# At the turn between the two parities: the last down matmuls ahead of the first key product, and the last chunk's weight sums two places sooner

## The chip, the cores and the metric

The kernel runs on one core of a Trainium2 chip. The metric is the device time of one execution in microseconds (us). The work is done by TensorE (PE in the profile; PEld is its weight load), VectorE (DVE), ScalarE (ACT), GpSimd (POOL) and SyncE (SP). POOL and SP here do hardly anything but issue DMA transfers.

## The reference

Out of one input x (2048 tokens, 512 wide) two branches are computed, and mixed per token by a gate.

```
def _A_ref(x, wqkv, wo):                      # 32 heads of 16, window of 8 tokens, every second one
    qkv = (x @ wqkv) -> q, k, v
    idx = pos[:, None] - 2 * arange(8)[None, :]
    logits = einsum("bhsd,bhswd->bhsw", q, k[idx]) * scale      # masked where idx < 0
    return einsum("bhsw,bhswd->bhsd", softmax(logits), v[idx]) @ wo

def _B_ref(x, w_gate, w_up, w_down):          # 1792 hidden columns
    return (gelu(x @ w_gate) * (x @ w_up)) @ w_down

g = sigmoid((x * gate_w).sum(-1))
return g * _A_ref(x, wqkv, wo) + (1 - g) * _B_ref(x, w_gate, w_up, w_down)
```

## The kernel before

**Parities.** The attention looks back over every second token, so the tokens are dealt into two halves of 1024, here called parities (`par` 0 and 1). The program runs in this order: `start()` makes the keys and queries of the first parity, `ffn(0)` makes its values and its whole feed-forward branch, `kq_second()` makes the keys and queries of the second parity, `ffn(1)` does the rest. The place where `ffn(0)` goes over into `kq_second()` is the turn.

**Products.** Each fp32 operand is split in a rounded part (`hi`) and the rest (`lo`), and a product is three matmuls: hi by hi, lo by hi, hi by lo. A group of products in two by two blocks is done with seven block products in place of eight (the names `a11`, `s1`, `t1` and so on are the block operands, where `s` and `t` are sums of blocks). An operand is made by one ScalarE copy for `hi` and one VectorE subtraction for `lo`. In `kq_second()` one such block product is `block(...)`: 24 matmuls. Its first is `a11` by `b11` into the four PSUM banks `acc0` to `acc3` (called `U`); ScalarE then copies the four banks into four banks of the tag `p` (called `V_`), and the second product, `a12` by `b21`, goes on top of these. The third, `s2` by `t2`, goes on top of `U`.

**Feed-forward.** `ffn(par)` goes over 14 chunks `f` of 128 hidden columns. `gate_up` does the seven products of a chunk, and between them, at nine places numbered 0 to 8, the steps that were put there with `at(place, step)`: fetches of later chunks' weights, sums of weight blocks (`combine`), their splits (`operands`, `down_w`), and pieces of the down product of the chunks before. The seventh product of a chunk (`last`, `a22` by `t4`) is done in the next chunk. `hidden` then makes gelu(gate) times up and splits it into `hh` and `hl`: a VectorE multiplication, a ScalarE rounding, a VectorE subtraction. `down` multiplies a pair of chunks' `hh` and `hl` with the down weights. Its tiles `b` = 0 stand in the banks `acc0` to `acc3` and its tiles `b` = 1 in `p` banks; at the last pair both are copied out with the scale `gc` (line 613), which frees the banks.

**Weights of a chunk, first parity.** Two chunks ahead, `fetch(f + 2)` loads the four weight blocks into a `raw` tile, and `combine(f + 2)` makes the sums `t1`, `t3`, `t2`, `t4` in place by three VectorE subtractions (line 499): first `t1` and `t3` in one instruction, then `t2`, then `t4`. One chunk ahead, `operands(par, f + 1, i)` makes, for the group of blocks `i` = 0 (`t1`, `t2`, `b11`) and `i` = 1 (`b21`, `t3`, `t4`, `b22`), a negated rounded copy on ScalarE (line 517), adds the raw weights to it by a DMA that accumulates, issued from POOL (line 518: `lo` is what this DMA leaves), and makes the rounded copy itself on ScalarE (line 522). So line 517 waits for `combine`, line 518 for line 517, and the first product of the chunk for the landing of line 518.

**What sets the order.** A scheduler decides the order of the instructions on each engine from a priority (the order in which the code records them) and its own estimate of times. The code bends it by hand: `paced(ins)` makes an instruction wait for the matmul recorded last; `ordered(a, b)` only fixes that `a` stands behind `b` on the same engine, with no semaphore. The helpers `row`, `act` and `mms` chain what is recorded through them on VectorE, ScalarE and TensorE in the order of the code; `mms` chains the matmuls of `block`. The attention itself (lines 325 to 401, VectorE for the most part) is a generator, `fill`, from which pieces are pulled in between at a lower priority.

**The turn.** After the chunks, `ffn(0)` records the last pair's `down` tiles, `b` = 0 and then `b` = 1, and after each of them one step of `ready()`, which makes operands for the second parity: `s12` sums, `b21`, `s1` and so on. Then `kq_second()` begins with its first block. In the built program, in which the down matmuls and the chained block matmuls bear no order to each other, the scheduler put the last twelve down matmuls (those of the 14th chunk's `hh` and `hl` by its down weights, four `p` tiles) behind the first block.

Of the kernel before, what the change touches and what calls it, by code (L numbers as in the profile page):

```python
# [12 lines left out]
AF = mybir.ActivationFunctionType  # L13
OP = mybir.AluOpType
# [8 lines left out]
FC = F // P  # L23
# [26 lines left out]
def tile_gated_mix(ctx: ExitStack, tc: tile.TileContext, xt, wqkv, wff, wo, out):  # L50
    nc = tc.nc
# [10 lines left out]
    def tl(tag, dt=F32):  # L62
        return pool.tile([P, COLS.get(tag, 512)], dt, name=tag, bufs=BUFS[tag])
# [12 lines left out]
    LAST, SCORED, PEAK, LESS = [], [], [], []  # L76
# [195 lines left out]
    def values(par):  # L272
        steps = [value_steps(par, t) for t in range(BT)]
        for chunk in PLAN:
            for place in chunk:
                for n in place.split():
                    steps[int(n[1])][n[0]]()
                    pull(0.77)
                if n == "g3":
                    done.add((par, 1))  # L280
                yield
# [127 lines left out]
    def after(ins, other, cls=mybir.DependencyClass.Sync):  # L409

        tc.add_manual_dep(ins.ins, other.ins.name, mybir.DependencyInfo(cls, mybir.DependencyReason.SCHED_ONLY),
                          reason="pace")

    def paced(ins):
        after(ins, LAST[-1])

    def ordered(ins, other):
        after(ins, other, mybir.DependencyClass.NoSync)
# [85 lines left out]
    def operands(par, f, i):  # L504


        n = len(GROUPS[i]) * QW
        w = tl(f"g{i}", F32R)
        hi, lo = w[:, :n], w[:, n:2 * n]
        for k, op in enumerate(GROUPS[i]):  # L510
            WG[f, op] = hi[:, k * QW:(k + 1) * QW], lo[:, k * QW:(k + 1) * QW]
        if par and not i:
            nc.sync.dma_start(w[:, :2 * n].bitcast(F32), WS[f, i])
            yield
            return
        raw = RAW[f][:, (0, 4)[i] * QW:][:, :n]
        nc.scalar.activation(lo, raw, AF.Copy, scale=-1.0)  # L517
        nc.gpsimd.dma_start(lo.bitcast(F32), raw, accum_op=OP.add)  # L518
        if not i:
            KEEP[f] = w[:, :2 * n]  # L520
        yield
        ins = nc.scalar.activation(hi, raw, AF.Copy)  # L522
        if f:
            paced(ins)

    def keep(f):

        WS[f, 1] = dram.tile([P, 2 * QW], F32, name=f"ws{f}1")
        paced(nc.sync.dma_start(WS[f, 1], RAW[f][:, 5 * QW:7 * QW]))
# [40 lines left out]
        return s  # L570

    def hidden(key, ge, up):
        nc.vector.tensor_tensor(ge, ge, up, op=OP.mult)  # L573
        hh_, hl_ = tl("hh", F32R)[:, :512], tl("hl", F32R)[:, :512]
        nc.scalar.activation(hh_, ge, AF.Copy)  # L575
        nc.vector.tensor_tensor(hl_, ge, hh_.bitcast(F32), op=OP.subtract)  # L576
        Hs[key] = hh_, hl_

    late, COPIED = [], []

    def pace(par, f):
        return PACE[2 if par else f > 5]
# [122 lines left out]
    def ffn(par):  # L705
        XOP.update(((n, kc), X[par, blk, kc + k]) for n, blk, k in (("a11", 0, 0), ("a12", 0, 2), ("a22", 1, 2))
                   for kc in range(2))
        todo, extra = iter(()), values(par)
        for f in range(FC):
            do = {}  # L710

            def at(i, x, *args):
                do.setdefault(i, []).append(lambda: x(*args))

            if f > 1:
                pieces = [[lambda b=b, i=i: down(par, f // 2 - 1, f % 2 * 2 + i, b)] for b in range(2) for i in range(2)]
            else:
                pieces = [()] * 4
            if f + 1 < FC:
                for i in range(2):  # L720
                    steps = operands(par, f + 1, i)
                    at(1 + 2 * i - (not par and f == 1), next, steps, None)
                    at(5 + i - (not par and f == 1), next, steps, None)
                if f:
                    at(0 if f != 1 else 7 if par else 5, fetch_d, f + 1)
                else:
                    for g_ in range(2):
                        at(6 + g_, fetch_d, g_)
                if f == 1:
                    for g_ in range(2):  # L730
                        at(3, down_split, g_)
                if f in (2, 3) and not par:
                    at(3 if f == 2 else 1, down_split, f)
                elif f > 1:
                    steps = down_w(f)
                    at(0 if f % 2 and not par else 2, next, steps, None)
                    at(7, next, steps, None)
            else:
                steps = down_w(f)
                at(1, next, steps, None)  # L740
                at(4, next, steps, None)
            if par:
                if f + 2 < FC:
                    at(0, fetch_sums, f + 2)
                else:
                    at(0, fetch_o) if f + 2 == FC else None
                if f + 1 == FC:
                    todo = chain(load_o(), channels_of(0, 0))
                    for i in range(1, 9):
                        at(i, next, todo, None)  # L750
            else:
                if f + 2 < FC:
                    at(1, fetch, f + 2)
                    at((4, 5, 6)[f] if f < 3 else 8, combine, f + 2)
                else:
                    at(0, fetch_x, 1, f + 2 - FC)
                if f + 1 < FC:
                    do.setdefault(0, []).insert(0, lambda: keep(f + 1))
                at(0, keep_parts, f)
                if f + 1 == FC:  # L760
                    todo = before()
                    for i in range(2, 9):
                        at(i, next, todo, None)
            gate_up(par, f, pieces, do, extra if f < 2 else iter(()))
        for _ in todo:
            pass
        fourth()
        if par:
            out_first()
            oT = {}  # L770
        else:
            Q2["mark"] = LAST[-1]
            Q2["turn"] = ready()
        for b in range(2):
            for t in range(BT):
                down(par, NG - 1, t, b)
                if par and t == 0:
                    oT[0, b] = channels(par, 0, b)
                if not par:
                    next(Q2["turn"], None)  # L780
        if par:
            finish(oT)
# [117 lines left out]
    row, act, mms = Row(nc.vector), Row(nc.scalar), Row(nc.tensor)  # L900
# [5 lines left out]
    SRC, OP_, Q2, RAWS = {}, {}, {}, {}  # L906
# [15 lines left out]
    def hi(n, k):  # L922
        return act.activation(OP_[n, k][0], SRC[n, k], AF.Copy)
# [16 lines left out]
    def block(ps, a, w, first, kcs=(0, 1), ask=0.0):  # L940
        for t in range(BT):
            for kc in kcs:
                ah, al = OP_[a, kc]
                wh, wl = OP_[w, kc]
                for n, (a_, w_) in enumerate(((ah, wh), (al, wh), (ah, wl))):
                    mm(ps[t], t, a_, w_, first and kc == 0 and n == 0, kc == 1 and n == 2)
            if ask:
                pull(ask)
# [275 lines left out]
    def ready():  # L1224

        q = Q2["q"] = [[XR[k][:, i * 512:(i + 1) * 512] for i in range(4)] for k in range(2)]
        load_pairs("t2")
        name("t3", pairs(slots("g0", 3) + slots("c", 1)), halves(RAWS["b12"]))
        yield
        hi("a12", 1)  # L1230
        lo("a12", 1)
        s12 = Q2["s12"] = [tl("r") for _ in range(2)]
        for n in ("s1", "s2", "s3", "s4"):
            for k in range(2):
                XOP[n, k] = pair("S")
            name(n, [XOP[n, k] for k in range(2)], s12 if n in ("s1", "s2") else [q[k][n == "s4"] for k in range(2)])
        name("a22", [X[1, 1, 2 + k] for k in range(2)], [q[k][3] for k in range(2)])
        for k in range(2):
            after(row.tensor_tensor(s12[k], q[k][2], q[k][3], op=OP.add), Q2["mark"])
        paced(hi("b21", 0))  # L1240
        lo("b21", 0)
        yield
        paced(hi("b21", 1))
        lo("b21", 1)
        yield
        both(hi, "s1")
        both(lo, "s1")
        yield
        for k in range(2):
            sub(s12[k], s12[k], q[k][0])  # L1250
        yield
        sub(RAWS["b12"], RAWS["b22"], RAWS["b12"])
        yield

    def kq_second():
        for _ in Q2["turn"]:
            pass
        q, s12 = Q2["q"], Q2["s12"]
        t4 = slots("g1", 4)
        name("t4", pairs(t4), halves(RAWS["b21"]))  # L1260
        U = [bank(f"acc{t}") for t in range(BT)]

        block(U, "a11", "b11", True, ask=ASK[0])
        V_ = [bank("p") for _ in range(BT)]
        for t in range(BT):
# [142 lines left out]
```

## Time and profile before

| | |
|---|---|
| Time, median of 3 runs | 598.41 us (597.75 to 599.1) |
| The profiled execution: its own time | 600.29 us |
| The profiled execution: span from first to last instruction | 598.5 us |
| Mean granted TensorE clock | 0.997 |
| Busy DVE / ACT / POOL | 539.8 / 389.7 / 87.6 us |
| HBM read / written | 68.30 / 38.86 MB |

Times in the views are microseconds from the span's start. In the views, `out<-in` names the tile written and the tiles read, `x4` is a count of merged instructions, and the bracket at a row's end is the time for which the engine was idle before it and what it waited for. The end of a matmul is modelled and reaches into the next one; the distance from one start to the next is the safe measure of its cost.

### The profile page before, as it was taken

The page shows a single profiled execution, that of the slowest core. Times are in us where ns is not written, and L with a number is a line of the kernel's source. Part 1 is how long each engine was busy: PE and PEld are TensorE (multiplying, and loading weights), DVE is VectorE, ACT ScalarE, POOL GpSimd, SP SyncE. Part 2 cuts the span into 40 slices and gives each one's busy share as a digit, 9 for nine tenths or more (in the row PEclk, how much of TensorE's full clock was granted, in tenths as well). Part 3 has the DMA queues.
Part 4 walks back from the last instruction along what each step waited for, and adds up shares of the span by engine and source line. Part 5 has one row for each costly group of instructions (what it writes and reads, how often), then busy time and mean ns, then how long its engine had stood idle before and what let it go on. Part 6 is the DMA issues. An engine that isn't in the chain of part 4 may idle for free.

```text
span 598.5 us, 8098 instructions
## 1 busy us (share of the span) xinstructions
PE 588.5 (98%) x2730; PEld 489.1 (82%) x2730; DVE 539.8 (90%) x646; ACT 389.7 (65%) x676; POOL 87.6 (15%) x119
## 2 busy tenths in 40 slices
PE   9999999999999999899899999999999999999997
PEld 6888988888888788787788988888788888888886
DVE  5998999879999899799899999998999999999972
ACT  5857656597677876686784446767656756695532
POOL 0501101021212121101108001111111111101200
PEclk9999999999999999999899999999999999999999
DMA  8778989788998898988669898876878878737834
GB/s 314 248 232 233 275 268 284 221 207 255 239 286 221 223 263 216 236 275 301 213 184 263 253 267 199 246 219 160 214 183 214 209 203 237 221 96 204 127 67 158
DMA packets 79522, 133.65 MB, mean 223 GB/s; under 512 B 7932, under 2 KB 45178, under 8 KB 79224
## 3 DMA queue, kind: packets, MB, share of 16 engines
q1 hardware_dynamic: 64426, 98.72, 50.6%
q0 software_dynamic: 12288, 32.45, 27.4%
q10 hardware_dynamic: 2766, 1.96, 1.0%
q8 instruction: 21, 0.34, 0.2%
q14 instruction: 21, 0.17, 0.1%
HBM read 68.30 MB, written 38.86 MB: 179 GB/s over the span
## 4 chain that ended last, share of the span: by engine, by line
PE 90%; DMA 3%; ACT 2%; DVE 2%; issue 2%; SPq 0%; POOL 0%; POOLq 0%; ACTq 0%; DVEq 0%
PE p L560 41%; PE p L602 11%; PE acc L602 11%; PE acc L898 7%; PE acc L211 7%; PE p L898 6%; PE p L831 5%; PE acc L831 2%; DMA g<-raw 2%; DMA prod<-wqkv 1%; DVE prod L388 1%; ACT g L517 0%; ACT L345 0%; ACT rt L613 0%; ACT L657 0%
## 5 line engine op out<-in xcount | busy, mean ns | idle before, releaser
L560 PE MATMUL p<-S,g 128*128 128x512 f32 x672 | 168.0, 390 | 0.6 <-DVE s L569 0.6
L560 PEld LDWEIGHTS p<-S,g 128*128 128x128 f32 x672 | 125.7, 188 | 26.9 <-DVE s L569 1.0
L560 PE MATMUL p<-A,g 128*128 128x512 f32 x504 | 128.8, 390 | 1.8 <-DMA g<-raw 1.8
L560 PEld LDWEIGHTS p<-A,g 128*128 128x128 f32 x504 | 93.5, 188 | 21.3 <-DMA g<-raw 2.3
L328 DVE TENSOR_REDUCE lg<-prod 128x128 f32<-128x2048 f32 x32 | 72.9, 2278 | 0.1
L518 POOL DMA_DIRECT2D g<-raw x40 | 34.5, 862 | 244.8 <-ACT g L517 130.7
L602 PE MATMUL p<-d,hh 128*128 128x512 f32 x224 | 68.3, 391 | 0.2 <-ACT p L596 0.2
L602 PE MATMUL acc<-d,hh 128*128 128x512 f32 x224 | 61.1, 389 | 0.0
L388 DVE TENSOR_TENSOR prod<-kq,lg 128x2048 f32<-128x2048 f32 x24 | 54.6, 2273 | 2.0 <-PE p L602 1.1
L602 PEld LDWEIGHTS p<-d,hh 128*128 128x128 f32 x224 | 41.7, 188 | 10.2 <-ACT p L596 1.7
L602 PEld LDWEIGHTS acc<-d,hh 128*128 128x128 f32 x224 | 42.1, 188 | 8.6
L565 ACT ACTIVATE s<-p 128x512 f32<-128x512 f32 x56 | 33.2, 596 | 24.3 <-PE p L560 24.0
L522 ACT ACTIVATE g<-raw 128x1024 fp32r<-128x1024 f32 (+1 forms) x40 | 39.5, 988 | 12.8 <-PE p L560 9.6
L618 ACT ACTIVATE rt<-p 128x512 f32<-128x512 f32 x48 | 27.7, 592 | 24.9 <-PE p L602 24.6
L569 DVE TENSOR_TENSOR s<-p,s 128x512 f32<-128x512 f32 x56 | 37.9, 680 | 6.0 <-PE p L560 5.4
L576 DVE TENSOR_TENSOR hl<-c,hh 128x512 fp32r<-128x512 f32 x56 | 38.1, 680 | 4.4 <-ACT hh L575 4.2
L602 PE MATMUL p<-d,hl 128*128 128x512 f32 x112 | 42.0, 389 | 0.0
L573 DVE TENSOR_TENSOR c<-c,s 128x512 f32<-128x512 f32 x56 | 38.1, 681 | 2.9 <-ACT c L676 2.9
L575 ACT ACTIVATE hh<-c 128x512 fp32r<-128x512 f32 x56 | 35.1, 626 | 8.7 <-DVE c L573 8.4
L517 ACT ACTIVATE g<-raw 128x1024 fp32r<-128x1024 f32 (+1 forms) x40 | 39.3, 986 | 1.3 <-DMA raw<-wff 0.5
L392 DVE TENSOR_TENSOR prod<-prod 128x1024 f32<-128x1024 f32 x32 | 38.9, 1216 | 0.2
L547 POOL DMA_DIRECT2D d<-r x22 | 18.9, 857 | 130.3 <-ACT d L546 93.2
(205 smaller groups left out, 1021.1 us busy)
## 6 DMA issues: line engine op xcount, KB each, us to landing
g<-raw POOLq DMA_DIRECT2D x27, 512.0 KB, 7.2
raw<-wff SPq DMA_DIRECT2D x42, 256.0 KB, 3.7
ws<-g SPq DMA_DIRECT2D x14, 768.0 KB, 6.3
g<-ws SPq DMA_DIRECT2D x14, 768.0 KB, 6.1
r<-wff SPq DMA_DIRECT2D x28, 256.0 KB, 4.0
d<-r POOLq DMA_DIRECT2D x22, 256.0 KB, 6.5
g<-raw POOLq DMA_DIRECT2D x13, 384.0 KB, 5.6
os<-tb SPq DMA_DIRECT2D x64, 64.0 KB, 4.3
```

What stands on the lines that cost most here:

```text
L211: LAST[:] = [nc.tensor.matmul(ps[:, :cols], x[:, ts], y, start=start and k == 0 and n == 0, stop=k == 1 and n == 2, skip_group_check=True)]
L328: nc.vector.tensor_reduce(two_of(lg, jj), prod.rearrange("p j w (h d) -> p (j w) h d", d=DH), axis=AX.X, op=OP.add)
L388: paced(nc.vector.tensor_tensor(prod.rearrange("p j w (h d) -> p (j w) h d", d=DH), spans(v, jj).rearrange("p j w (h d) -> p j w h d", d=D ...
L392: nc.vector.tensor_tensor(prod[:, :, :4], prod[:, :, :4], prod[:, :, 4:], op=OP.add)
L517: nc.scalar.activation(lo, raw, AF.Copy, scale=-1.0)
L522: ins = nc.scalar.activation(hi, raw, AF.Copy)
L560: LAST[:] = [nc.tensor.matmul(ps, w_, a_, start=(start and kc == 0 and n == 0), stop=(kc == 1 and n == 2), skip_group_check=True)]
L573: nc.vector.tensor_tensor(ge, ge, up, op=OP.mult)
L576: nc.vector.tensor_tensor(hl_, ge, hh_.bitcast(F32), op=OP.subtract)
L602: ins = nc.tensor.matmul(pp, a[:, ts], w, start=(i == 0 and n == 0 and gr == 0), stop=(i == 1 and n == 2), skip_group_check=True)
L831: ins = nc.tensor.matmul(pa, a, b, start=(first and n == 0), stop=(last and n == 2), skip_group_check=True)
L898: return lambda *args, **kw: self.add(getattr(self.eng, name)(*args, **kw))
```

## The change

Two things are changed.

First, `combine(13)`, the weight sums of the last chunk, is recorded in the twelfth chunk (`f` = 11) at place 6 instead of place 8.

Second, at the turn: `hidden` keeps its multiplication and its rounding in two lists, so that `ready()` can put the first `s12` sum behind the last multiplication on VectorE, and the first rounding of `b21` behind the last rounding on ScalarE; and before the first block of `kq_second()` the chain of block matmuls is tied to the last down matmul.

```diff
     def hidden(key, ge, up):
-        nc.vector.tensor_tensor(ge, ge, up, op=OP.mult)
+        MULTIPLIED[:] = [nc.vector.tensor_tensor(ge, ge, up, op=OP.mult)]
         hh_, hl_ = tl("hh", F32R)[:, :512], tl("hl", F32R)[:, :512]
-        nc.scalar.activation(hh_, ge, AF.Copy)
+        ROUNDED[:] = [nc.scalar.activation(hh_, ge, AF.Copy)]
         nc.vector.tensor_tensor(hl_, ge, hh_.bitcast(F32), op=OP.subtract)
...
-                    at((4, 5, 6)[f] if f < 3 else 8, combine, f + 2)
+                    at((4, 5, 6)[f] if f < 3 else 6 if f + 3 == FC else 8, combine, f + 2)
...
         for k in range(2):
-            after(row.tensor_tensor(s12[k], q[k][2], q[k][3], op=OP.add), Q2["mark"])
-        paced(hi("b21", 0))
+            ins = row.tensor_tensor(s12[k], q[k][2], q[k][3], op=OP.add)
+            after(ins, Q2["mark"])
+            ordered(ins, MULTIPLIED[0])
+        ins = hi("b21", 0)
+        paced(ins)
+        ordered(ins, ROUNDED[0])
...
+        mms.last = LAST[-1]
         block(U, "a11", "b11", True, ask=ASK[0])
```

No instruction is added or taken away; the order changes on the engines at two places.

**The last chunk's sums, VectorE.** `raw_2249` holds the last chunk's weights; the row with `2x256` makes `t1` and `t3`, the first row with `256` makes `t2`. Before:

```order
L569 TENSOR_TENSOR s_2288<-p_2260,s_2288 128x512
L328 TENSOR_REDUCE lg_2182<-prod_2252 128x16x8
L569 TENSOR_TENSOR s_2267<-p_2237,s_2267 128x512
L573 TENSOR_TENSOR c_2306<-c_2306,s_2288 128x512
L499 TENSOR_TENSOR raw_2249<-raw_2249 128x2x256
L325 TENSOR_TENSOR prod_2309<-v_612,kq_264 128x2048
L499 TENSOR_TENSOR raw_2249<-raw_2249 128x256
```

And of the change, from the same first row on:

```order
L569 TENSOR_TENSOR s_2288<-p_2260,s_2288 128x512
L499 TENSOR_TENSOR raw_2249<-raw_2249 128x2x256
L328 TENSOR_REDUCE lg_2182<-prod_2252 128x16x8
L569 TENSOR_TENSOR s_2267<-p_2237,s_2267 128x512
L573 TENSOR_TENSOR c_2306<-c_2306,s_2288 128x512
L499 TENSOR_TENSOR raw_2249<-raw_2249 128x256
L325 TENSOR_TENSOR prod_2309<-v_612,kq_264 128x2048
```

The sum `t2`, on which the copy of line 517 waits, now stands ahead of a long attention product (L325) instead of behind it. On ScalarE that copy (`g0_2372` is the first group of the last chunk) moves with it. Before:

```order
L639 ACTIVATE p_2370<-p_2363 128x512
L575 ACTIVATE hh_2336<-c_2306 128x512
L565 ACTIVATE s_2390<-p_2383 128x512
L546 ACTIVATE d_2392<-r_2230 128x512
L676 ACTIVATE c_2401<-p_2237 128x512
L596 ACTIVATE p_2446<-rt_1128 128x512
L517 ACTIVATE g0_2372<-raw_2249 128x768
```

And of the change:

```order
L639 ACTIVATE p_2370<-p_2363 128x512
L575 ACTIVATE hh_2339<-c_2306 128x512
L517 ACTIVATE g0_2372<-raw_2249 128x768
L565 ACTIVATE s_2390<-p_2383 128x512
L546 ACTIVATE d_2392<-r_2230 128x512
```

It moves ahead of four others; on POOL the accumulating DMA of line 518 for `g0_2372` likewise moves ahead of the one of line 547 for `d_2392`.

**The turn, TensorE.** A piece of the difference, with the rows of the change marked + and those of before marked -; `acc_2758` to `acc_2761` is the first block of the second parity, `p<-d,hh` and `p<-d,hl` are the down matmuls, `p<-g_2565,A` begins the second block:

```order
 L602 MATMUL p<-d,hl 128x512
+L602 MATMUL p<-d,hh 128x512 x8
+L602 MATMUL p<-d,hl 128x512 x4
 L898 MATMUL acc_2758<-g_2528,A 128x512 x6
 L898 MATMUL acc_2759<-g_2528,A 128x512 x6
 L898 MATMUL acc_2760<-g_2528,A 128x512 x6
 L898 MATMUL acc_2761<-g_2528,A 128x512 x6
-L602 MATMUL p<-d,hh 128x512 x8
-L602 MATMUL p<-d,hl 128x512 x4
 L898 MATMUL p<-g_2565,A 128x512 x5
```

The twelve down matmuls move from behind the first block to ahead of it. **On VectorE** `c_2629` and `hl_2633` are the last chunk's multiplied hidden tile and its rest, `r_2664` and `r_2665` the `s12` sums. Before, the multiplication stood behind the two sums, and from it on the rows are these:

```order
L573 TENSOR_TENSOR c_2629<-c_2629,s_2520 128x512
L396 TENSOR_TENSOR o_2487<-prod_2597 128x4x64
L401 STREAM_TRANSPOSE tb_2486<-o_2487 128x512
L898 TENSOR_TENSOR g0_2565<-S_2567,g0_2565 128x512
L898 TENSOR_TENSOR c_2566<-S_2567,g0_2565 128x512
L898 TENSOR_TENSOR S_2666<-r_2664,S_2666 128x512
L898 TENSOR_TENSOR S_2667<-r_2665,S_2667 128x512
L898 TENSOR_TENSOR r_2664<-r_2664,raw_2358 128x512
L898 TENSOR_TENSOR r_2665<-r_2665,raw_2490 128x512
L898 TENSOR_TENSOR S_2563<-S_2586,S_2563 128x1024
L576 TENSOR_TENSOR hl_2633<-c_2629,hh_2632 128x512
```

Of the change, from the same row on:

```order
L573 TENSOR_TENSOR c_2629<-c_2629,s_2520 128x512
L898 TENSOR_TENSOR r_2664<-raw_2358 128x512
L898 TENSOR_TENSOR r_2665<-raw_2490 128x512
L396 TENSOR_TENSOR o_2487<-prod_2597 128x4x64
L576 TENSOR_TENSOR hl_2633<-c_2629,hh_2632 128x512
L401 STREAM_TRANSPOSE tb_2486<-o_2487 128x512
L898 TENSOR_TENSOR g0_2565<-S_2567,g0_2565 128x512
L898 TENSOR_TENSOR c_2566<-S_2567,g0_2565 128x512
L388 TENSOR_TENSOR prod_2719<-kq_264,lg_1588 128x2048
```

The rest `hl_2633` moves ahead of eight rows, and the two sums behind the multiplication. On ScalarE the rounding `hh_2632` moves from the last place of nine to the second, right behind the copy of the first `acc` bank (line 613). On SP three of the four stores of line 403 stand ahead of the last load of `t1` (line 976), and the fourth behind it.

More of the change, by code (lines that the diff above doesn't have):

```diff
@@ L572, in hidden @@
     def hidden(key, ge, up):
-        nc.vector.tensor_tensor(ge, ge, up, op=OP.mult)
+        MULTIPLIED[:] = [nc.vector.tensor_tensor(ge, ge, up, op=OP.mult)]
         hh_, hl_ = tl("hh", F32R)[:, :512], tl("hl", F32R)[:, :512]
-        nc.scalar.activation(hh_, ge, AF.Copy)
+        ROUNDED[:] = [nc.scalar.activation(hh_, ge, AF.Copy)]
         nc.vector.tensor_tensor(hl_, ge, hh_.bitcast(F32), op=OP.subtract)
         Hs[key] = hh_, hl_
-    late, COPIED = [], []
+    late, COPIED, MULTIPLIED, ROUNDED = [], [], [], []
     def pace(par, f):
```

## Prediction

> **What bounds the kernel now.** First the busy shares, then what TensorE waited for:
>
> ```profile
> PE 588.5 (98%) x2730; PEld 489.1 (82%) x2730; DVE 539.8 (90%) x646; ACT 389.7 (65%) x676; POOL 87.6 (15%) x119
> ...
> PE p L898 <- ACT p L898: 2.3, 1, 2.3
> PE p L560 <- DMA g<-raw: 1.8, 1, 1.8
> PE p L560 <- DVE s L569: 0.6, 1, 0.6
> ```
>
> TensorE is busy 98% of the span and waits for others hardly at all; only three waits past the start are worth naming (total, times, longest). So time can be won only in those waits, or where its matmuls run slower than usual. The usual pace is read at the turn, in the timeline of TensorE:
>
> ```profile
> 250.56 0.61 PE L560 MATMUL p<-A,g 128*128 128x512 f32 x2
> 253.00 1.20 PE L560 MATMUL p<-A,g 128*128 128x512 f32 x4 [1.83 <-DMA g<-raw]
> 254.04 0.62 PE L602 MATMUL p<-d,hl 128*128 128x512 f32 x2
> ...
> 275.15 5.60 PE L898 MATMUL acc<-g,A 128*128 128x512 f32 x24
> 280.60 1.98 PE L602 MATMUL p<-d,hh 128*128 128x512 f32 x8
> 282.41 1.07 PE L602 MATMUL p<-d,hl 128*128 128x512 f32 x4
> 285.80 2.35 PE L898 MATMUL p<-g,A 128*128 128x512 f32 x5 [2.32 <-ACT p L898]
> ...
> 292.98 5.60 PE L898 MATMUL acc<-d,S 128*128 128x512 f32 x24
> ```
>
> The first block's 24 matmuls take 280.60 - 275.15 = 5.45 us from start to start, 0.227 each. Against this pace two places lose time.
>
> At the turn, 275.15 to 292.98 is 17.83 us for 24 + 12 + 24 = 60 matmuls, which at 0.227 are 13.62: **4.21 us lost**. Of it, 285.80 - 282.41 - 4 x 0.227 = 2.48 is the gap, and 7.18 - 5.45 = 1.73 is the second block's slower pace. The chain of waits tells what made the gap:
>
> ```profile
> 242.62 10.34 DMA g<-raw
> ...
> 282.83 0.69 ACT rt L613 x2
> ...
> 285.25 0.50 ACT p L898
> ```
>
> The last down matmuls end, ScalarE frees their four `p` banks (L613), copies the first bank of `U` over (L898), and only then can the second block begin. The slower pace shows in the granted clock: first the page's row of 40 slices, then the view of single stretches (busy us of PE, PEld, DVE, ACT and POOL, then the clock, the DMA share and GB/s).
>
> ```profile
> PEclk9999999999999999999899999999999999999999
> ...
> 252.00:253.00 1.00, 0.00 (x0) 0.00 (x0) 0.00 (x0) 0.00 (x0) 0.00 (x0) 1.00 1.02 202
> 286.00:287.00 1.00, 1.00 (x3) 0.79 (x3) 0.96 (x2) 1.00 (x3) 0.09 (x1) 0.50 0.90 309
> 289.00:290.00 1.00, 1.00 (x4) 0.79 (x4) 0.13 (x1) 1.00 (x3) 0.00 (x0) 0.79 1.01 390
> ```
>
> After the gap the clock is at half until about 289.4 (0.79 over a stretch that began at 0.50). That is the only slice of the page with less than 9; in the other gap, at 252, the clock stays at 1.00.
>
> At the last chunk, 250.56 to 254.04 is 3.48 us for six matmuls, 1.36 at the pace: **2.12 us lost**. There TensorE, and with it every engine (row 252 to 253), waits for the accumulating DMA issued at 242.62, which takes 10.34 us.
>
> **The change, part 1: the last chunk's sums.** No instruction is added; three VectorE sums and what hangs on them move.
>
> ```profile
> 236.84 0.68 DVE L499 TENSOR_TENSOR raw<-raw 128x512 f32<-128x512 f32 x1
> 237.45 2.29 DVE L325 TENSOR_TENSOR prod<-v,kq 128x2048 f32<-128x2048 f32 x1
> 239.65 0.42 DVE L499 TENSOR_TENSOR raw<-raw 128x256 f32<-128x256 f32 x1
> ...
> 241.50 0.83 ACT L517 ACTIVATE g<-raw 128x768 fp32r<-128x768 f32 x1
> ...
> DMA to landing us min/median/max: 4.2/6.4/11.0
> ```
>
> In the new order `t2` stands where L325 began, so it ends at about 237.45 + 0.42 = 237.9. ScalarE's copy L517, now third behind L639 and L575 there, starts at about 238.1 in place of 241.50, and the DMA goes out 3.4 us sooner, at about 239.2 instead of 242.62. TensorE needs the landing at 250.56 + 2 x 0.227 = 251.0, so the DMA has 11.8 us. The last row is the landing of all 40 DMAs of L518: the slowest took 11.0. With its own 10.34 it lands at 249.6. So I take the whole 2.12 us as gone; the bounds are 0 (it lands as late as before) and 2.12. What is late next is the second group's DMA, which goes out sooner too, because its copy no longer stands behind so much. On POOL the down weights' DMA changes places with it and goes out right behind it, for a product that is still a chunk away. On TensorE the last product of the chunk before moves behind three others; nothing there is added, and I cost it at nothing.
>
> **Part 2: the turn.** The same 60 matmuls in the order 12, 24, 24. The second block's `p` banks are then freed and filled while the first block's 5.45 us run. The times here are those of before, without part 1's shift.
>
> ```profile
> 271.87 1.29 DVE L898 TENSOR_TENSOR r<-raw 128x512 f32<-128x512 f32 x2
> 274.27 0.68 DVE L573 TENSOR_TENSOR c<-c,s 128x512 f32<-128x512 f32 x1
> 281.06 0.68 DVE L576 TENSOR_TENSOR hl<-c,hh 128x512 fp32r<-128x512 f32 x1
> ...
> 272.06 0.60 ACT L676 ACTIVATE c<-p 128x512 f32<-128x512 f32 x1
> 274.00 0.69 ACT L613 ACTIVATE s<-acc,gc 128x512 f32<-128x512 f32 x1 [0.70 <-PE acc L602]
> 278.38 0.64 ACT L575 ACTIVATE hh<-c 128x512 fp32r<-128x512 f32 x1
> 276.76 1.16 ACT L898 ACTIVATE S<-r 128x512 fp32r<-128x512 f32 x2
> 282.83 2.42 ACT L613 ACTIVATE rt<-p,gc 128x512 f32<-128x512 f32 x4 [3.81 <-PE p L602]
> 285.13 1.09 ACT L898 ACTIVATE p<-acc 128x512 f32<-128x512 f32 x2
> ...
> 285.16 1.23 DVE L392 TENSOR_TENSOR prod<-prod 128x1024 f32<-128x1024 f32 x1
> ```
>
> The down matmuls now need `hh` at 275.15 and `hl` eight matmuls later, at 277.0. The multiplication (L573) loses the two sums ahead of it: 274.27 - 1.2 = 273.1, after gelu's end at 272.7; it ends at 273.75. The rounding (L575) stands behind the first L613 of ScalarE (274.00, and 0.6 to the next start, as four take 2.42) and ends at about 275.2: TensorE loses **0.1**. `hl` follows the two sums (1.2) and one row of 256 columns (0.4, as the second L499), starts at about 275.3 and ends at 276.0, 1.0 ahead of need. Queued behind the rounding on ScalarE are the copies of the other three `acc` banks; the second of them is needed at 279.3, when the block reaches it.
>
> The first block then runs from 277.95 to 283.4. From 275.2 ScalarE has three `acc` copies and four roundings, seven rows at 0.6 with a few waits on TensorE and VectorE, until about 279; then the four L613 (2.42) until 281.3 and the first two bank copies (1.09) until 282.4: ahead of 283.4. The third and fourth bank copies stand behind the `s2` roundings, which wait for VectorE's `r` sums, now behind a product L388 (2.29); I get 285.1 for the third against a need at 283.4 + 2 x 1.36 = 286.1, again 1.0 to spare. So the gap goes, and with it the half clock. Gain 4.21 - 0.1 = **4.1 us**.
>
> What is late next is VectorE.
>
> ```profile
> 250.00:300.00 50.00, 45.85 (x193) 36.82 (x192) 42.42 (x57) 34.41 (x62) 6.07 (x10) 0.97 0.75 251
> ...
> 302.88 1.88 DVE L898 TENSOR_TENSOR g<-S,g 128x512 fp32r<-128x512 f32 x3
> ...
> 303.86 5.60 PE L898 MATMUL acc<-g,A 128*128 128x512 f32 x24
> ...
> 310.85 2.29 DVE L388 TENSOR_TENSOR prod<-v,lg 128x2048 f32<-128x2048 f32 x1 [1.28 <-PE p L898]
> ```
>
> It has 42.4 us of work in these 50 us, which become 43.8: 1.4 us are left. Its idle time was the two gaps. Laid out row by row with the durations of before, it runs up to 0.8 us later against TensorE than it did (my estimate). The tightest need is the fourth block (303.86), whose sixth matmul wants the second `g` split: that ended at 303.56 with 1.4 us to spare; 0.7 remain. At 310.85 VectorE waited 1.28 us for TensorE, and there it has caught up. Behind that, TensorE's only wait is the 0.6 of the first list, which I leave.
>
> **Sum.** 2.1 + 4.1 = 6.2 us. The profiled execution's 600.29 us become 594.1 (span 598.5 to 592.3). The median of the runs is 598.41, 1.88 below the profiled execution; the same 6.2 off gives **592.2 us**.
>
> **The page on the clock.** The Trainium skill, TensorE: Matmul & The Clock Gate, section "Part 1: The HAM clock gate", says that the clock falls to half after at least one idle window of about 3.4 us, and comes back after as long a busy one. The length agrees: half clock from 286.0 to 289.4. The cause doesn't: here the gap before it was 2.5 us. Taken at its word, the gap is too short, the half clock has another cause, and it would stay. The rows decide for me, and the rule stands beside the fourth rival.
>
> **The rivals.**
>
> 1. *The DMA is late anyway.* For: while it runs the DMA engines are full, and what counts may be when all that was asked for is moved, not when this one was asked for:
>
> ```profile
> 244.00:248.00 4.00, 4.00 (x19) 3.34 (x18) 4.00 (x4) 4.00 (x6) 0.43 (x1) 1.00 1.01 331
> ```
>
> Against: by its new time it is asked for ahead of a load and a store that it was behind. Then 4.1 alone is won: 594.3.
>
> 2. *VectorE becomes the bound at the turn.* For: 97% of the stretch. One L388 with the L392 behind it (2.29 + 1.23) ahead of a split that a block needs costs 3.5 less the 0.7 spare, 2.8: 595.0.
>
> 3. *Slower: the last hidden tile stands uncovered.* The first block used to run while `hl` was made (281.06 to 281.74). If its VectorE rows, whatever the written order, come as late as they did, TensorE waits from 277.0 to 281.7, 4.7, and at half clock loses 1.7 more: 6.4, which eats the gain (598.6). With one L388 and L392 more ahead of it, 3.5, it is 602. Slower by what can be told, 1.2, needs a loss of 7.4, a wait of 5.7 beside the clock: it decides from `hl` at about 282.7. Against: gelu's end at 272.7 and the printed order.
>
> 4. *The half clock isn't the gap's.* For: the other gap, of 2.0 us, left the clock at 1.00. Against: the half clock comes right behind this gap, 2.5 long, and nowhere else on the page. It would follow the second block to its new place: 1.7 of the 6.2 isn't won, 593.9.
>
> 5. *The moves don't take effect*, or an equal wait opens elsewhere: 598.4. Against: the order shows both moves.
>
> **Chances.** Forecast 0.74, DMA late 0.08, VectorE 0.08, slower 0.03, half clock 0.03, no effect 0.04. About 0.2% (1.2 us) is what can be told from no change. Faster: 0.74 + 0.08 + 0.08 + 0.03 = 0.93; same 0.04; slower 0.03. The range takes in the forecast, the rivals at 594.3 and 593.9, and VectorE's at 595.0; below, the 0.6 us wait on VectorE might go as well, and the runs spread by 0.6 each way: 591.0 to 595.0.
>
> **What would show it.** Right: the chain passes the turn from L602 to L898 with no ScalarE step; the second block takes 5.45 us from start to start at clock 1.00; the six matmuls of the last chunk's start take 1.4 us; the DMA of its first group goes out near 239. Wrong: a wait of TensorE for `hh` or `hl` (L575, L576) ahead of the first block, for a split (L898 on VectorE) in the second to fourth block, or for `g<-raw` near 250; or a larger wait on VectorE's L569 in place of the 0.6.

## The result and the profile after

| | before | change |
|---|---|---|
| Time, median | 597.95 us (5 runs, 596.90 to 599.10) | 595.05 us (5 runs, 594.62 to 595.42) |
| Ratio, 95% interval | | 0.9949 [0.9934, 0.9964] |
| The profiled execution: time / span | 600.29 / 598.5 us | 595.18 / 593.4 us |
| Mean granted clock in it | 0.997 | 1.000 |

The change is faster, by 2.9 us where 6.2 were forecast. The profiled executions differ by 5.1 us, so much of the shortfall lies in what the one execution of before stood for. The page after, busy shares and the row of the clock:

```profile
PE 587.1 (99%) x2730; PEld 487.8 (82%) x2730; DVE 539.8 (91%) x646; ACT 390.0 (66%) x676; POOL 87.6 (15%) x119
...
PEclk9999999999999999999999999999999999999999
```

The one slice at 8 is gone. The waits of TensorE after, past the start (total, times, longest):

```profile
PE p L560 <- DVE s L569: 0.6, 1, 0.6
PE acc L898 <- DVE A L898: 0.4, 1, 0.4
PE p L602 <- ACT p L596: 0.3, 1, 0.3
```

Both large waits of before, on `p` (2.3) and on `g<-raw` (1.8), are gone, and none as large has come. Now the timeline of TensorE after, first the last chunk's start, then its seventh product and the turn:

```profile
250.65 1.52 PE L560 MATMUL p<-A,g 128*128 128x512 f32 x6
252.00 0.61 PE L602 MATMUL p<-d,hl 128*128 128x512 f32 x2
...
268.34 1.65 PE L560 MATMUL p<-A,g 128*128 128x512 f32 x6
...
273.69 0.39 PE L602 MATMUL p<-d,hl 128*128 128x512 f32 x1
274.01 2.14 PE L602 MATMUL p<-d,hh 128*128 128x512 f32 x8
275.99 1.08 PE L602 MATMUL p<-d,hl 128*128 128x512 f32 x4
276.90 5.60 PE L898 MATMUL acc<-g,A 128*128 128x512 f32 x24
282.35 1.29 PE L898 MATMUL p<-g,A 128*128 128x512 f32 x5
...
287.81 5.60 PE L898 MATMUL acc<-d,S 128*128 128x512 f32 x24
```

Before, the seventh product stood here:

```profile
269.71 1.52 PE L560 MATMUL p<-A,g 128*128 128x512 f32 x6
```

At the turn the same 60 matmuls take 287.81 - 274.01 = 13.80 us, before 17.83: 4.03 won. The six matmuls of the last chunk's start take 1.35 in place of 3.48. But from that start to the seventh product, 250.65 to 268.34, it is 17.69 us, and before 250.56 to 269.71 = 19.15: only 1.46 of the 2.13 won at the start are left 18 us later. The chain of waits of the change shows where the rest went:

```profile
254.85 5.25 DMA raw<-xt
...
260.18 0.63 ACT A L898
...
261.84 1.28 ACT L345
263.12 0.01 issue
263.13 0.64 ACT lg L345
...
265.08 2.20 DVE prod L388
...
267.74 0.56 DVE s L569
268.30 0.04 issue
268.34 1.65 PE p L560 x6
```

The chain now leaves TensorE and runs over a load of x (L109), ScalarE's copy of it (L898), the exponential (L345, whose first 1.28 us are the loading of its table) and VectorE to the seventh product. ScalarE idles 0.96 us ahead of that copy. Why the load is late stands in SyncE's waits and its timeline, both of the change, and in the landing of the second group's accumulating DMA (L518):

```profile
SPq L109 <- DMA ws<-raw: 22.7, 2, 13.6
```

```profile
240.15 0.38 SPq L535 DMA_DIRECT2D ws<-g  x1
240.62 0.52 SPq L529 DMA_DIRECT2D ws<-raw  x1
254.85 1.23 SPq L109 DMA_DIRECT2D raw<-xt  x2
```

```profile
L518 POOL DMA_DIRECT2D g<-raw x1: 856/856/856, 245.0 to 245.0; - x1
...
DMA to landing us min/median/max: 9.5/9.5/9.5
```

The load goes into a `raw` tile that the last chunk's weights leave, and SyncE holds it back until these have been read: by the second group's DMA, which lands at 254.5, and, a little later still, by the store of the sums (L529). That store goes out at 240.62 and lands 14.1 us later, at 254.7:

```profile
L529 SPq DMA_DIRECT2D ws<-raw x1: 519/519/519, 240.6 to 240.6; - x1
...
DMA to landing us min/median/max: 14.1/14.1/14.1
```

Before it went out at 243.83 and took 8.4, so that the load waited for the second group's DMA alone (out at 247.57, landed after 7.9 us, at 255.5):

```profile
243.83 0.32 SPq L529 DMA_DIRECT2D ws<-raw  x1
255.56 1.21 SPq L109 DMA_DIRECT2D raw<-xt  x2
```

With the sums made earlier, the store goes out right behind a store of 768 KB (L535, 240.15) and beside the first group's accumulating DMA.

### The profile page after: what moved, and what is told of

Its sections match the earlier page's. It is cut to its first block, busy times and chain, and to the rows that moved or that the text cites. A ratio compares the mean times of both kernels' runs of the same rounds, so it can differ in the third digit from the quotient of the medians.

```text
span 593.4 us, 8099 instructions
## 1 busy us (share of the span) xinstructions
PE 587.1 (99%) x2730; PEld 487.8 (82%) x2730; DVE 539.8 (91%) x646; ACT 390.0 (66%) x676; POOL 87.6 (15%) x119
## 4 chain that ended last, share of the span: by engine, by line
PE 89%; ACT 4%; DMA 3%; DVE 3%; issue 1%; ACTq 0%; SPq 0%
PE p L560 41%; PE acc L602 12%; PE p L602 11%; PE acc L898 7%; PE acc L211 6%; PE p L898 6%; PE p L831 6%; PE acc L831 2%; DMA raw<-xt 2%; DMA r<-wff 1%; DVE prod L388 1%; ACT L345 1%; ACT g L517 0%; ACT A L898 0%; DVE s L569 0%
## 5 line engine op out<-in xcount | busy, mean ns | idle before, releaser
L518 POOL DMA_DIRECT2D g<-raw x40 | 34.5, 863 | 252.8 <-ACT g L517 157.7
L575 ACT ACTIVATE hh<-c 128x512 fp32r<-128x512 f32 x56 | 35.1, 627 | 9.4 <-DVE c L573 9.2
L602 PE MATMUL acc<-d,hl 128*128 128x512 f32 x112 | 36.9, 389 | 0.0
```

Of the source, the lines that this page charges most:

```text
L602: ins = nc.tensor.matmul(pp, a[:, ts], w, start=(i == 0 and n == 0 and gr == 0), stop=(i == 1 and n == 2), skip_group_check=True)
```

## The experiments

Three theories stood at the start. **A:** the wait for the accumulating DMA differs between executions, and the profiled one had a long one; part 1 (the sums) is worth 0 to 0.7 us and part 2 (the turn) 2.5 to 4. **B:** that wait is usual and part 1 worth it; the turn was priced too high. **C:** both parts are worth what was worked out, but together they make new waits between 261 and 268 that take it back. From e5 on, A also says what part 1 ran into: a crowd of transfers that it only moves. D and E are told in the expectations.

### e1: the sums alone

```diff
-                    at((4, 5, 6)[f] if f < 3 else 8, combine, f + 2)
+                    at((4, 5, 6)[f] if f < 3 else 6 if f + 3 == FC else 8, combine, f + 2)
```

> Part 1 alone: only the last chunk's sums two places sooner. The timed gain of the whole change was 2.9 us where the two profiled executions differ by 5.1 in span. Theory A (the DMA wait of 2.1 us at the last chunk was a matter of the one profiled execution of before, and the usual execution hardly has it): 0 to 0.7 us faster than before. Theory B (the wait is usual, and it is the turn that was priced too high): 1.8 to 2.4 us faster. Its profile has no wait for g<-raw near 250 under either.

Measured: 598.84 us (12 runs) against 598.62 of before, ratio 0.9991 [0.9973, 1.0009]. Part 1 alone wins nothing that can be told. Its profile has no `g<-raw` wait, but it has the new one. ScalarE in its timeline:

```profile
260.12 0.63 ACT L898 ACTIVATE A<-raw 128x512 fp32r<-128x512 f32 x1 [1.08 <-DMA raw<-xt]
```

So the wait near 260 needs no change at the turn, which goes against C.

### e2: the turn alone

The edits at the turn, as the change has them; the sums stay at place 8.

> Part 2 alone: only the turn's order. Theory A: 2.5 to 4 us faster than before, nearly all of the change's gain. Theory B: 0.5 to 1.5 us. Theory C (both parts are worth what was worked out, but together they make new waits between 261 and 268, some 0.7 us, and more elsewhere): 3.8 to 4.3 us faster here and 1.8 to 2.4 in the run of part 1 alone, more together than the change gave.

Measured: 594.98 us (12 runs), ratio 0.9939 [0.9919, 0.9959]: all of the change's gain, 3.6 us against the runs of before beside it. B falls with it. Its waits of TensorE show no `g<-raw` either, though the sums are late: the first group's DMA went out at 242.2, as before, and landed in 7.6 us instead of 10.3. Its last chunk, from the first matmul to the seventh product, loses nothing:

```profile
250.17 1.52 PE L560 MATMUL p<-A,g 128*128 128x512 f32 x6
...
267.20 1.55 PE L560 MATMUL p<-A,g 128*128 128x512 f32 x6
```

### e3: before, once more

> The kernel before once more, for a second profiled execution. Theory A: the wait of TensorE for g<-raw near 251 is under 1 us or gone, the landing of that DMA under 9.5 us, the span near 596.2; the gap at the turn is 2.3 us again, with half clock behind it. Theory B: the wait is 1.8 us again, and the gap or the half clock at the turn is smaller.

Measured: the profiled execution took 597.06 us, span 595.3. The gap at the turn is the same, but the second block isn't slowed. Its timeline of TensorE, then the view of stretches (busy us of PE, PEld, DVE, ACT and POOL, the clock, the DMA share, GB/s):

```profile
251.28 1.19 PE L560 MATMUL p<-A,g 128*128 128x512 f32 x4 [0.59 <-DMA g<-raw]
...
284.08 1.43 PE L898 MATMUL p<-g,A 128*128 128x512 f32 x5 [2.32 <-ACT p L898]
...
289.73 5.60 PE L898 MATMUL acc<-d,S 128*128 128x512 f32 x24
```

```profile
286.00:287.00 1.00, 1.00 (x6) 0.78 (x6) 0.93 (x2) 1.00 (x4) 0.00 (x0) 1.00 1.08 354
```

The block takes 289.73 - 284.08 = 5.65 us against 7.18 in the first profile, at clock 1.00 where that showed 0.50, and the DMA wait is 0.59 against 1.83. Two of the three prices that the forecast took from one execution are thus not those of the next one of the same kernel.

### e4: the tie without the two orderings

Only the last line of the change, `mms.last = LAST[-1]`: the down matmuls go first, but nothing keeps the `s12` sums behind `hidden`'s multiplication nor the `b21` rounding behind its rounding.

```diff
+        mms.last = LAST[-1]
         block(U, "a11", "b11", True, ask=ASK[0])
```

> The turn with the tie of the block matmuls to the last down matmul alone: the multiplication, rounding and subtraction of the last hidden tile stay where they were on VectorE and ScalarE. This is the third rival of the prediction made real: TensorE is to wait for hh and hl ahead of the first block, 3 to 5 us from about 275, with half clock behind it; time 0 to 3 us over that of before. If hh and hl come in time without their new places, the gain is the same as with the turn alone, and the two ordered() lines do nothing. On VectorE the scheduler also reorders rows of the values behind 313, so a difference under 0.5 us says nothing.

Measured: 600.83 us (10 runs), ratio 1.0036 [1.0017, 1.0056], slower. TensorE at the turn, then the clock:

```profile
278.25 3.52 PE L602 MATMUL p<-d,hh 128*128 128x512 f32 x8 [3.75 <-ACT hh L575]
...
282.52 5.60 PE L898 MATMUL acc<-g,A 128*128 128x512 f32 x24
```

```profile
278.00:279.00 1.00, 0.75 (x2) 0.66 (x3) 1.00 (x2) 0.19 (x1) 0.51 (x1) 0.50 1.03 370
```

The last hidden tile's rounding (L575) now stands behind the operands of the second parity on ScalarE, TensorE waits 3.75 us for it, and the clock drops here too. This is the forecast's third rival made real: the orderings are what makes the tie pay.

### e5: the change, with a store out of the way

The 768 KB store of the split operands of the 13th chunk (`f` = 12; L535) is put behind the second x load. The expectation calls it chunk 10's; the edit, which acts where `f + 2 == FC`, moves the one of `f` = 12, out at 240.15 in the change.

```diff
-                at(0, keep_parts, f)
+                at(8 if f + 2 == FC else 0, keep_parts, f)
```

> The change with one more edit: the 768 KB store of chunk 10's kept sums (L535, out of SyncE at 240.2 in the profile of the change) goes out after the second x load instead of ahead of it. Theory A (the sums' transfers meet a crowd in the queues, and making them earlier only moved the crowd on to the second x load): with the store out of the way the first sums' transfer (L518, 10.2 us with the change) lands in 6 to 8 us, the second x load leaves before 253, ScalarE no longer waits for that load ahead of its copy at 260 (L898, 1.0 us with the change), the last chunk's second a22 product starts 0.5 to 0.8 us sooner (268.34 with the change), and the median is 594.0 to 594.6. Theory D (the crowd is not this store's; the second x load is late for its place behind the first group's reads of the raw tile): landing 9 to 10.5 us, the wait at 260 stays, the median is that of the change, 594.8 to 595.4.

Measured: 594.10 us (5 runs, 593.78 to 594.50), ratio to before 0.9921 [0.9898, 0.9945]; the change run beside it (e7) 595.02 (594.77 to 595.57), so the runs of the two don't overlap. SyncE's timeline, ScalarE's and TensorE's:

```profile
240.47 0.33 SPq L529 DMA_DIRECT2D ws<-raw  x1
252.03 1.21 SPq L109 DMA_DIRECT2D raw<-xt  x2
```

```profile
259.03 0.62 ACT L898 ACTIVATE A<-raw 128x512 fp32r<-128x512 f32 x1
```

```profile
267.60 1.55 PE L560 MATMUL p<-A,g 128*128 128x512 f32 x6
```

The L529 store goes out at the same time as in the change and lands in 8.1 us, not 14.1; the x load leaves 2.8 us sooner; ScalarE's wait is gone; the seventh product starts 0.74 sooner. What the x load waits for last is now the second group's DMA, and it too is faster, 7.0 us instead of 9.5:

```profile
SPq L109 <- DMA g<-raw: 11.1, 1, 11.1
```

```profile
L518 POOL DMA_DIRECT2D g<-raw x1: 856/856/856, 244.9 to 244.9; - x1
...
DMA to landing us min/median/max: 7.0/7.0/7.0
```

That DMA is issued from POOL, so it isn't only the place behind L535 on SyncE's own queue that made the transfers long. The first group's landing missed its number, 8.7 us where 6 to 8 were expected; it isn't this store that sets it, for with the store in place it took 10.2 us in the change, but 7.3 in e1 and 7.5 in e7. Theory A's numbers otherwise held, D's did not.

### e6: the turn alone, with the store out of the way

The same line for the store, the sums at place 8.

> The turn's part alone with the same store moved behind the second x load, the sums as before. Theory A: the transfer of the first sums lands in 6 to 8 us in every execution, so the wait of 0 to 2.1 us that it left at TensorE in some executions is gone without part 1: 594.2 to 594.9. Theory D: as the turn alone, 594.7 to 595.3, and the landing takes 7.6 to 10.3 us.

Measured: 593.91 us (6 runs, 593.51 to 596.44), ratio 0.9924 [0.9901, 0.9946], a little under the expected 594.2. The first group's DMA landed in 7.0 us. With the queues relieved the earlier sums add nothing: e5 and e6 can't be told apart.

### e7: the change again

> The change itself again, beside the kernel before on the same chip. Theory A: 594.8 to 595.4, ratio 0.993 to 0.996, and, since the gap at the turn is 0.4 us or less, none of its executions has a mean clock of 0.997 or less but for stretches elsewhere (before: about half have one window at half clock). The profile shows ScalarE's wait for the second x load ahead of its copy near 260 again (0.5 to 1.2 us). Theory E (that wait was this one profiled execution's): no such wait, and the second a22 product of the last chunk starts near 267.5.

Measured: 595.02 us (5 runs), ratio 0.9939 [0.9918, 0.9960]. ScalarE's wait came again, as long:

```profile
259.98 0.63 ACT L898 ACTIVATE A<-raw 128x512 fp32r<-128x512 f32 x1 [0.99 <-DMA raw<-xt]
```

So E falls: the wait is there in all three profiles with the earlier sums (e1, the change, this one). It isn't theirs alone, though. e4, with the sums as before, has it too:

```profile
260.60 0.63 ACT L898 ACTIVATE A<-raw 128x512 fp32r<-128x512 f32 x1 [1.02 <-DMA raw<-xt]
```

No run of the change, in 10, has a mean clock under 0.999.

### e8: the orderings without the tie

The turn's edits without the `mms.last` line, the sums at place 8.

> The turn's part without the line that ties the last down product ahead of the first block (mms.last), sums as before: the two ordered value rows stay, and the scheduler lets rows of the first key block stand between the down products. Theory A (the gain is the gap filled by the down products in any order ahead of VectorE's and ScalarE's results): time of the turn alone within 0.5 us, 594.5 to 595.5, and no gap over 0.7 us at the turn. Rival (the rows between push the last down products behind, the accumulator banks come free later and the second block waits): 596 to 598, with a TensorE wait of 1 to 3 us at the second or third block.

Measured: 595.76 us (6 runs, 595.00 to 596.37), ratio 0.9948 [0.9928, 0.9968], between the two expectations and, by the intervals, not told apart from e2. TensorE at the turn:

```profile
275.37 1.52 PE L898 MATMUL acc<-g,A 128*128 128x512 f32 x6
276.73 1.98 PE L602 MATMUL p<-d,hh 128*128 128x512 f32 x8
278.54 1.52 PE L898 MATMUL acc<-g,A 128*128 128x512 f32 x6
279.90 1.07 PE L602 MATMUL p<-d,hl 128*128 128x512 f32 x4
...
288.99 5.60 PE L898 MATMUL acc<-d,S 128*128 128x512 f32 x24
```

With the two rows ordered, the scheduler itself takes the down matmuls in between the rows of the first block, and the same 60 matmuls, 275.37 to 288.99, take 13.62 us: no loss at all. The rival's wait at the second or third block didn't come. That its times lie above e2's isn't shown to come from the turn: in its profile the last chunk begins at 251.85, 1.7 us later than in e2, with fewer matmuls done in the first 20 us, and it has a `g<-raw` wait of 0.58.

## Why the prediction was right or wrong

**The turn: right, row by row.** TensorE loses 274.01 - 273.69 - 0.227 = 0.1 us for `hh`, as forecast. The chain passes the turn with no ScalarE step, the second block takes 287.81 - 282.35 = 5.46 us, and no wait on VectorE has come there, so the second rival (VectorE as the bound) didn't happen. The measured time, 595.05, is that rival's 595.0 and with it the top edge of the stated range, but by chance: the rival's mechanism isn't in the trace. The turn in the profiled pair gave 4.03 for 4.1.

**The half clock: right in the profile, mis-sized for the median.** The term of 1.73 us was read from an execution that had it, and taken off a median over executions of which only some have it. A window of half clock lowers the mean clock of a run by 3.4 x 0.5 / 598 = 0.003. Of the 40 runs of before that stand beside the experiments, 21 show 0.997 or less. So the term is worth, as an estimate, about 21/40 x 1.73 = 0.9 us to a typical run. The times agree: these 21 runs take 599.4 us on average and the other 19 take 598.0, a difference of 1.5 us. Gap 2.48, less 0.1, plus 0.9 makes 3.3 for the turn; measured alone, 3.6, with an interval (0.9919 to 0.9959) of 2.5 to 4.8. That the half clock hangs on the gap is borne out: of the 39 timed runs without the gap (the change, e2, e5 to e8) 2 show 0.997 or less, and none of the change's 10; of the 62 with it (before, e1, e4) 38 do, and 9 of the 10 of e4, with the longer gap. The fourth rival falls.

**The last chunk's sums: the step that failed.** The DMA was forecast to go out at 239.2 and land at 249.6; it went out at 239.32 and landed 10.2 us later (7.3 and 7.5 in e1 and e7), and the six matmuls take 1.35 us against 1.36. What failed is the price, 2.12 us, and the sentence that what is late next, the second group's DMA, goes out sooner too. The price was the worst of several executions. A measure for all profiles is the time from the first matmul of that chunk to its seventh product, 17.0 in the three that lost nothing there:

| | from a11 to a22 | lost there | to |
|---|---|---|---|
| sums as before: before, e3, e4, e8 | 19.15, 17.92, 17.88, 17.94 | 2.1, 0.9, 0.9, 0.9 | `g<-raw`, e4 mostly the x load |
| sums as before: e2 | 17.03 | 0 | |
| sums sooner: e1, change, e7 | 17.80, 17.69, 17.73 | 0.8, 0.7, 0.7 | the x load |
| store moved: e5 (sums sooner), e6 (as before) | 17.04, 17.03 | 0 | |

With the sums as before the loss is 0.95 us on average over the five, with the sums sooner 0.71: 0.2 us won in place of 2.12, which isn't told from nothing. The issues went out sooner, but into a crowd. The second group's DMA left at 244.8 to 245.0 in the three profiles with earlier sums, and at 247.1 to 248.9 in before, e2, e3, e4 and e8; but it took 9.4 to 9.5 us against 5.1 to 7.9, and landed at 254.2 to 254.5, later than in e2, e3 and e4 (252.3 to 253.8; 255.5 in before and e8). The L529 store, let out 1 to 3 us sooner than in before, took 14.1, 12.1 and 12.0 us against 6.6 to 8.4, and landed at 254.5 to 254.7. Both read the `raw` tile, which so came free late, and the next x load went out late with it. What is late next was looked for among what waits for the sums on TensorE's side; it was the tile's next writer, on SyncE's queue. e5 shows that the crowd is the cause: without the 768 KB beside them the same store takes 8.1 us and the same DMA 7.0, and the loss is gone.

**The sum.** 6.2, less 1.9 for the sums and 0.8 for the half clock, is 3.5 us; the two timings of the change gave 2.9 (595.05 against 597.95) and 3.9 (595.02 against 598.91). By the profiled pair, where the half clock counts in full, the forecast of 6.2 stands against 5.1. The first rival (the DMA late anyway) had the right size for the sums and the wrong reason: the DMA did come in time, and the transfers behind it were late.

**What stays open.** Which runs of before had a long `g<-raw` wait can't be read from their times; the mean of 0.95 rests on five profiles of four orders of the turn. The mean clock of a timed run doesn't say where its half clock lies; only the profiles of before, e1 and e4 show it at the turn. Why the first group's DMA took 10.2 us in the change and 7.3 and 7.5 in e1 and e7 isn't shown. And two of e2's 12 runs had a mean clock of 0.997 though the gap was gone; no profile caught one.

## What to carry to other kernels

A wait read from one profiled execution is one draw: profile the same kernel again before pricing a wait that hangs on a crowded DMA, or a clock that answers to a gap; here both shrank at once. When a step is moved earlier, follow all it releases, the stores and the next writer of its tile too; here, with the DMA engines full, the store and the second group's DMA were issued sooner and took so much longer that the next load gained nothing, and moving another store out of the stretch did what moving the issue could not. An order between matmuls that needs late operands is worth nothing without the order of those operands on their engines: the tie alone cost 2.2 us, the two orderings alone gave most of the gain.

## What the runs showed of the hardware

The half clock after a gap was a matter of chance here. With a TensorE wait of 2.32 us it followed in one profile of before and in e1, and not in e3; the mean clock of the timed runs of before says 21 of 40. After the wait of 3.75 us it was 9 of 10. In before and in e4 it lasted about 3.4 us (286.0 to 289.4, and 277.9 to 281.3 in e4's stretches). The Trainium skill, TensorE: Matmul & The Clock Gate, section "Part 1: The HAM clock gate", says that the window of about 3.4 us runs freely, which agrees with the chance and the length; that a whole idle window is needed, these runs contradict, since a gap of 2.3 to 2.5 us was enough about half of the time by the mean clock, and in two of three profiles.

The landing of one DMA, L518 of the last chunk's first group (384 KB), issued at the same place in the program, took 10.3, 9.1, 9.1, 8.3 and 7.6 us in before, e3, e8, e4 and e2, with the DMA engines full throughout (mean share 0.97 to 1.02 from 240 to 250).
